# A second expert of 320 rows instead of 384, and the last stage's weight parts made beside the last experts

## The chip, the cores and the metric

One core of one Trainium2 chip runs the whole program: TensorE (PE) multiplies, VectorE (DVE), ScalarE (ACT) and GpSimd (POOL) do the rest, and SyncE (SP), ACT and POOL issue DMAs. The metric is the device time of one execution in microseconds (us); lower is better. In the profile PEld is the loading of a stationary operand, and ACTq, POOLq and SPq are the places from which DMAs are issued.

## The reference

Three layers follow one another, all in float32:

```python
# 1. attention, 2 x 8 heads, 1152 keys, 576 pooled queries, head 64
q_pool = q.reshape(B, H, S // 2, 2, D).mean(axis=3)
attn = softmax(q_pool @ k.T / sqrt(D));  x = attn @ v          # x: 1152 rows x 512
# 2. eight experts, each row goes to the one with the largest logit
e_idx = argmax(x @ w_gate);  gate_w = softmax(...)[e_idx];  eom = sigmoid(x @ w_output_gate)
for e in range(8):
    h = maximum(x[mask] @ w1[e], 0)                            # 512 -> 1024
    out[mask] = gate_w[mask] * eom[mask, e] * (h @ w2[e])      # 1024 -> 512
# 3. a gated layer
h = x @ w_in                                                   # 512 -> 2048
y = (h * tanh(softplus(h))) @ w_out                            # 2048 -> 512
```

With the inputs that the reference draws, the experts have, from the largest to the smallest, 374, 267, 240, 69, 63, 61, 51 and 27 rows.

## The kernel before

**Precision.** A product of two float32 matrices is made of three faster products (`mm3`, L1021): each operand is split into a high part `...h` and a low part `...l` (ACT copies the high part, DVE or POOL subtracts it to get the low part), and high x high, low x high and high x low are summed in PSUM. A small matrix is multiplied directly as four-byte values, without a split, in two halves of 64 columns of the array (`mm2_half`, L1039): with m = 64 rows the left half of the array makes output columns 0 to 255 and the right half 256 to 511.

**Stages.** Attention lasts to about 262 us, routing (`routing_rest`, `routing_over`) to about 285 us with the first expert begun at 278 us, then the eight experts run as "slots" one after the other to 423.5 us, and the last stage runs from 428.9 us to the end.

**Experts.** The routing ranks them by their number of rows, and `CAP` (L34) says how many groups of 64 rows the program holds for each rank: 6, 6, 4, 2, 1, 1, 1, 1. A rank with more rows than its place overflows into a loop at the end. `order` (L872) puts the ranks into slots: 0, 3, 4, 1, 5, 2, 6, 7. So slot 3 is the second largest expert (place for 384 rows), slot 5 the third (256), slots 1, 2, 4, 6 and 7 are narrow. On PE slot 3 runs from 337.3 to 372.9 us, slot 4 to 382.1, slot 5 to 406.9, slot 6 to 415.4 and slot 7 to 423.4.

A wide slot (`wide_slot`, L1105) gathers its rows in chunks of 128, transposes them, and then runs steps i = 0 to 9. Step i < 8 makes one of eight blocks of 128 hidden columns: 12 products `hps` into a PSUM buffer (there are two), of n = 384 columns in slot 3; then `relu` (L1015): ACT makes `hh` and DVE `hl`. Step i >= 2 adds, for k = i - 2, the block's part of the second layer: three products `yp` of 512 columns for each chunk of 128 rows. Two steps ahead, `w1split` (POOL makes the low part from the fourth block on) and `w2split` (ACT and DVE) split the weights into rings of four buffers, `w1h`, `w1l`, `w2h`, `w2l`; the raw weights `wt` come by four DMAs of 1 MB for an expert into five buffers. A narrow slot with 64 rows multiplies four-byte values from `wt` and splits nothing.

**Decoding and last stage.** The last stage's weights lie in memory packed and are decoded on the way (`decode_step`: DVE operations `ds`, `dm`, `wd`, an ACT copy `dm`) into 16 buffers `wd` of 1024 columns; `DECS` (L1256) says how many of these half steps follow each step of slots 0 to 4. They too are split, `wh` by ACT (`split_hi`, L1237) and the low part by DVE in place of `wd` (`split_lo`). `NPRE` = 5 of the 16 are split in slots 5 and 6, the other eleven in the last stage's steps 0 to 11.

The last stage takes three blocks of 384 rows, each in 16 steps. Step f multiplies 12 products `zps` (384 columns), evaluates the gate (ACT exp and logarithm; DVE `n`, `l`, `l`, `n`, `gl`, `n`; POOL `u`), and, four steps later (`LAG`), adds 9 products `ops` (512 columns). What each engine does in a step, and in which order, stands in the list `order_` (L1483). Between experts and last stage `turn` (L1070) brings the reloaded rows `xl<-ybuf` into PSUM, scaled by DVE (`rescale`), and `add_rows` (L1100) adds the last two experts' rows, which `pick` has prepared.

Each engine works through its own instructions in program order, and the order is that of the code: no scheduler moves anything.

Of the kernel before, what the change touches and what calls it, by code (L numbers as in the profile page):

```python
# [32 lines left out]
CAPW = 3  # L33
CAP = (6, 6, 4, 2, 1, 1, 1, 1)  # L34
# [50 lines left out]
def kernel(ctx, tc, cst, qt, kt, v, wgo, w1, w2, wio, out):  # L85
# [733 lines left out]
    astack.close()  # L819
    mstack = ExitStack()  # L820
# [101 lines left out]
    def routing_over():  # L922

        cap, nc9, ov, b8, inc = rt("cap", [8]), rt("nc9", [8, 9]), rt("ov", [8]), rt("b8", [8, 8]), rt("inc", [8])
        ts(V, cap, pi_, -1.0, ALU.mult, float(CAPW + 1), ALU.add)
        ts(V, cap, cap, float(CAPW), ALU.min, 0.0, ALU.max)

        ch, cr = rt("ch", [8]), rt("cr", [8])
        ts(V, ch, pi_, -2.0, ALU.mult, 7.0, ALU.add)
        ts(V, ch, ch, 5.0, ALU.min, 0.0, ALU.max)  # L930
# [70 lines left out]
    def split(name, w, bufs, eng):  # L1001
        hi = mp_.tile([P, 4, P], F32R, name=name + "h", bufs=bufs)
        lo = mp_.tile([P, 4, P], F32R, name=name + "l", bufs=bufs)
        act(hi, w)
        tt(eng, lo, w, hi.bitcast(F32), ALU.subtract)
        return hi, lo
# [4 lines left out]
    def w2split(s, k):  # L1011
        h_, l_ = split("w2", w2t[s, k // 4][:, k % 4].rearrange("p (a b) -> p a b", b=P), 4, V)
        w2s[s, k] = h_.rearrange("p a b -> p (a b)"), l_.rearrange("p a b -> p (a b)")

# [17 lines left out]
    def evac_half(s, y=None, r=0):  # L1032

        y = mp_.tile([P, DM], F32, name="y", bufs=3) if y is None else y
        for d in range(2):
            act(y[r:r + 64, 256 * d:256 * d + 256], ypt[s, 0][64 * d:64 * d + 64, :256])
        return y

    def mm2_half(s, k, js):  # L1039
        if k == 0:  # L1040
            ypt[s, 0] = yps.tile([P, 4, P], F32, name="yp").rearrange("p a b -> p (a b)")
        w = w2t[s, k // 4][:, k % 4]
        for d in range(2):
            mm(ypt[s, 0][64 * d:64 * d + 64, :256], lhsT=hh[s, k // 4][:, js], rhs=w[:, 256 * d:256 * d + 256], start=k == 0, stop=k == 7)

# [59 lines left out]
    def wide_slot(s, cks):  # L1105
        n = len(cks) * P

        def xprep(j):
# [3 lines left out]
            ps = xpose(cks[j], *(((yps, "yp") if s == slots[0][0] else (fp[0], f"yb{j - 1}")) if j else ()))  # L1112
            js = slice(j * P, (j + 1) * P)
# [15 lines left out]
        def main(i):  # L1129
            if i < 8:  # L1130
# [11 lines left out]
                relu(s, i, ps[:, :n], n)  # L1142
            if i >= 2:
                k = i - 2
                for j, c in enumerate(cks):
# [87 lines left out]
    NPRE = 5  # L1233
    ws2 = {}


    def split_hi(b_, f):  # L1237
        if b_ == 0:
            pool, n = (wq[0], NPRE) if f < NPRE else (zp, NF - NPRE)
            hi = pool.tile([P, 1024], F32R, name="wh", bufs=n)  # L1240
            ws2[f] = [hi]
            act(hi, wd[f])

    def split_lo(b_, f, eng=V):
        if b_ == 0:
            lo = cp.tile([P, 1024], F32R, name="wd", bufs=16) if f else wq[0].tile([P, 1024], F32R, name="wl0")
            tt(eng, lo, wd[f], ws2[f][0].bitcast(F32), ALU.subtract)
            ws2[f].append(lo)

    HB = 3  # L1250
    RL, RS = [0, 5]
# [4 lines left out]
    DECS = [[0] * 5 + [1] * 4 + [2], [0] * 5 + [1], [0] * 6, [1, 0, 0] + [1] * 7, [1] * 5 + [0]]  # L1256
# [5 lines left out]
    allc = [(c, min(P, 64 * CAP[p_])) for p_, cks in slots for c in cks]  # L1262
# [30 lines left out]
    for q, (n_, i, _, main, w_, _) in enumerate(flat):  # L1293
# [30 lines left out]
        if q > RQ and n_ < len(DECS):  # L1324
            dp_ = dq[0] if dq else scratch
            for _ in range(DECS[n_][i]):
# [6 lines left out]
        elif wq and (n_ == 5 and i % 2 or n_ == 6 and i in (2, 3)) and len(ws2) < NPRE:  # L1333
# [49 lines left out]
    def zmm(b_, f):  # L1383
        fifth = (b_, f) == steps[LAG]
        ps = zt[b_, f] = (tps if fifth else zps).tile([P, 512], F32, name="tps" if fifth else "zps")
        h_, l_ = ws2[f]
# [54 lines left out]
    def omm(b_, f):  # L1441
        h_, l_ = ws2[f]
        wo, wl_ = h_[:, 512:], l_[:, 512:]
# [34 lines left out]
    def on(i, fn):  # L1478
# [4 lines left out]
    order_ = [(-1, z_exp), (-3, z_gate), (-2, z_inv), (-3, z_hi), (-2, z_newton), (-3, z_lo), (-1, z_num), (NPRE - 1, split_lo), (NPRE, split_hi)]  # L1483
    stages = {
        0: [(NPRE, split_hi)],
# [34 lines left out]
    def over_rows(ov):  # L1520
# [38 lines left out]
        for q in range(NF // 4):  # L1559
            ps = zps.tile([P, 512], F32, name="zps")  # L1560
            for i in range(4):
                a, b_ = ws2[4 * q + i]
# [12 lines left out]
            for i in range(4):  # L1575
                a, b_ = (x_[:, 512:] for x_ in ws2[4 * q + i])
# [59 lines left out]
```

## Time and profile before

| | us |
|---|---|
| median of 3 runs (lowest, highest) | 651.24 (649.33, 652.01) |
| the profiled execution | 648.99 |
| its span on the core | 647.1 |
| PE busy in it | 618.0 |
| DVE busy | 486.1 |
| ACT busy | 396.4 |
| POOL busy | 254.5 |

The profile shows one execution. 1.9 us of its time lie outside the span. A row of the timeline gives start, duration, engine, line, operation, output and inputs; in brackets at its end stands the idle time just before it on its engine and what ended that idle time. Because matmuls are pipelined, a row's duration is longer than the distance to the next one; what a matmul costs in a full stream is read from the distance between starts.

### The profile page before, as it was taken

How to read it: one execution, taken by the hardware profiler on the slowest of the kernel's cores; microseconds unless marked ns; L12 is line 12 of the kernel's file. 1: busy time of each engine (PE TensorE's matmuls, PEld its weight loads, DVE VectorE, ACT ScalarE, POOL GpSimd, SP SyncE). 2: the span in 40 equal slices, each digit the busy share in tenths (PEclk: the TensorE clock that was granted, in tenths of full speed). 3: DMA queues.
4: the chain of work that ended last, by engine and by line, in shares of the span. 5: the costliest groups of instructions: out<-in, count | busy, mean ns of one | idle time of the engine just before them, and what ended most of it. 6: DMA issues, size and time to landing. Idle time of an engine off the chain costs nothing.

```text
span 647.1 us, 11371 instructions
## 1 busy us (share of the span) xinstructions
PE 618.0 (96%) x4144; PEld 496.3 (77%) x4144; DVE 486.1 (75%) x995; ACT 396.4 (61%) x841; POOL 254.5 (39%) x235
## 2 busy tenths in 40 slices
PE   7999999999999999589999999999999999999996
PEld 4667778787787776279868868697879999999993
DVE  4667797978787879558847778249998778878775
ACT  7789888887887675244555367346655545454453
POOL 6747638384664342242215035103223332323221
PEclk8999999999999999699999999999999999999999
DMA  6956655364451332498798496820000200000001
GB/s 248 322 152 207 174 179 125 109 189 147 120 191 34 123 86 66 132 325 305 247 389 316 172 351 238 318 81 0 2 0 1 95 5 1 2 32 18 1 0 52
DMA packets 27405, 89.86 MB, mean 139 GB/s; under 512 B 2886, under 2 KB 7631, under 8 KB 23250
## 3 DMA queue, kind: packets, MB, share of 16 engines
q1 hardware_dynamic: 22176, 74.80, 32.6%
q0 software_dynamic: 3568, 8.79, 5.9%
q10 hardware_dynamic: 1602, 5.51, 2.6%
q8 instruction: 34, 0.56, 0.4%
q14 instruction: 25, 0.20, 0.1%
HBM read 79.65 MB, written 9.97 MB: 138 GB/s over the span
## 4 chain that ended last, share of the span: by engine, by line
PE 66%; DVE 15%; ACT 7%; issue 5%; DMA 3%; POOL 2%; SPq 0%; ACTq 0%; DVEq 0%; POOLq 0%
PE pv L341 10%; PE ops L1454 8%; PE mx L237 5%; PE sc L324 5%; PE sc L322 5%; DVE l L97 4%; DVE n L97 3%; DMA wt<-in_w 3%; PE zps L1023 3%; PE pv L373 3%; PE zps L1024 3%; PE zps L1025 3%; PE yp L1023 3%; PE yp L1025 2%; PE yp L1024 2%
## 5 line engine op out<-in xcount | busy, mean ns | idle before, releaser
L100 POOL TENSOR_SCALAR u<-u 128x384 f32<-128x384 f32 x46 | 58.2, 1265 | 147.0 <-ACT u L91 147.0
L91 ACT ACTIVATE pt<-sc 128x320 f32<-128x320 f32 (+1 forms) x198 | 87.8, 490 | 10.7 <-PE sc L322 7.9
L341 PE MATMUL pv<-pt,vt 128*64 128x288 f32 x576 | 75.6, 411 | 0.0
L91 ACT ACTIVATE l<-n,two 128x384 f32<-128x384 f32 x48 | 29.6, 617 | 74.6 <-DVE n L97 74.6
L103 DVE TENSOR_REDUCE Mp<-mx 128x1 f32<-128x384 f32 x72 | 40.1, 556 | 39.6 <-PE mx L237 34.6
L324 PE MATMUL sc<-qs,at 128*128 128x320 f32 (+1 forms) x264 | 67.4, 299 | 0.0
L322 PE MATMUL sc<-qb,Bt 66*128 66x320 f32 (+1 forms) x264 | 66.6, 296 | 0.0
L1023 PE MATMUL zps<-yh,wh 128*128 128x384 f32 x184 | 63.0, 343 | 1.8 <-DVE n L97 1.8
L1025 PE MATMUL zps<-yl,wh 128*128 128x384 f32 x184 | 61.9, 337 | 0.0
L341 PEld LDWEIGHTS pv<-pt,vt 128*64 128x64 f32 x576 | 39.0, 137 | 28.5 <-issue 5.2
L1024 PE MATMUL zps<-yh,wd 128*128 128x384 f32 x176 | 59.1, 336 | 0.0
L1454 PE MATMUL ops<-wh,gl 128*128 128x512 f32 x144 | 56.9, 400 | 1.4 <-DVE gl L94 0.8
L1454 PE MATMUL ops<-wh,gh 128*128 128x512 f32 x144 | 57.2, 397 | 0.9 <-ACT gh L91 0.9
L1454 PE MATMUL ops<-wd,gh 128*128 128x512 f32 x135 | 53.2, 394 | 0.0
L100 POOL TENSOR_SCALAR dm<-dm 128x512 f32<-128x512 f32 x21 | 41.5, 1977 | 23.1 <-ACT dm L91 23.0
L94 POOL TENSOR_TENSOR Bt<-kd,at 64x576 fp32r<-64x576 f32 x32 | 45.7, 1442 | 4.2 <-ACT at L91 4.1
L324 PEld LDWEIGHTS sc<-qs,at 128*128 128x128 f32 x264 | 46.2, 189 | 1.1 <-issue 0.8
L97 DVE SCALAR_TENSOR_TENSOR l<-n,r 128x384 f32<-128x384 f32 x48 | 26.7, 556 | 25.6 <-ACT r L91 25.6
L322 PEld LDWEIGHTS sc<-qb,Bt 66*128 66x128 f32 x264 | 45.3, 189 | 0.0
L1023 PEld LDWEIGHTS zps<-yh,wh 128*128 128x128 f32 x184 | 34.6, 188 | 4.6 <-DVE n L97 3.1
L237 PE MATMUL mx<-at,qs 128*128 128x384 f32 x120 | 35.7, 363 | 2.3 <-DVE qs L94 0.8
L1053 POOL DMA_INDIRECT ybuf<-y,six x11 | 11.2, 1020 | 66.2 <-ACT y L91 48.4
(327 smaller groups left out, 1615.0 us busy)
## 6 DMA issues: line engine op xcount, KB each, us to landing
wt<-in_w SPq DMA_DIRECT2D x32, 1024.0 KB, 8.0
kd<-in_kt SPq DMA_DIRECT2D x16, 576.0 KB, 5.3
wraw<-in_wio SPq DMA_DIRECT2D x11, 512.0 KB, 4.6
wd<-in_wio SPq DMA_DIRECT2D x11, 512.0 KB, 4.1
vt<-in_v SPq DMA_DIRECT2D x8, 576.0 KB, 5.7
wraw<-in_wio ACTq DMA_DIRECT2D x7, 512.0 KB, 5.8
tq<-in_qt SPq DMA_DIRECT2D x12, 288.0 KB, 4.4
tq<-in_qt POOLq DMA_DIRECT2D x12, 288.0 KB, 6.0
```

The lines of the kernel that those rows point to most:

```text
L91: A.activation(out=out, in_=in_, func=func, **kw)
L94: eng.tensor_tensor(out=out, in0=a, in1=b, op=op)
L97: V.scalar_tensor_tensor(out=out, in0=a, scalar=s, in1=b, op0=op0, op1=op1)
L100: eng.tensor_scalar(out=out, in0=a, scalar1=s1, scalar2=s2, op0=op0, op1=op1)
L237: mm(ps, lhsT=QS[p, h][:, j * P:(j + 1) * P], rhs=keys(h), start=True, stop=True)
L322: mm(o, lhsT=Bt[(2 * p + h) % NBL][:66, ks], rhs=QB[p, h][:66, qs_], start=False, stop=last_, skip_group_check=not (first and last_))
L324: mm(o, lhsT=At[p, h][:, ks], rhs=QS[p, h][:, qs_], start=first, stop=False, skip_group_check=not (first and last_))
L341: mm(pvt[p][f][64 * h:64 * h + 64, :HQ], lhsT=vt[p][:, t, h, :], rhs=Pt[p, t][:, h, f * HQ:(f + 1) * HQ], start=t == 0, stop=t == KT - 1, ...
L1023: mm(out_, lhsT=a, rhs=c, start=first, stop=False)
L1024: mm(out_, lhsT=b_, rhs=c, start=False, stop=False)
L1025: mm(out_, lhsT=a, rhs=d, start=False, stop=last_)
L1454: mm(opt[b_, j], lhsT=(g_, g_, gl_)[i], rhs=(wo, wl_, wo)[i], start=f == 0 and i == 0, stop=f == NF - 1 and i == 2)
```

## The change

Two things are changed, and two small ones with them.

- `CAP` of the second expert goes from 6 to 5 groups of 64 rows. Slot 3 then has n = 320 columns in its first layer. Its first 256 rows go on as before. The last 64 rows get their hidden values from ACT as four-byte values `ht` (128x64 for each of eight blocks), and `mm2_tail` multiplies them with the raw weights `wt`, 16 products of 256 columns in the two halves of the array, in two groups of eight: at step i = 5 (blocks 0 to 3) and i = 9 (blocks 4 to 7). `routing_over` computes the places by the new rule.
- The rings `w1h`, `w1l`, `w2h`, `w2l` move to a pool `wsp` that outlives the experts. Of the last stage's 16 weights f, 0 to 3 are split in slot 5 and 6 into `wh` as before, 4 to 11 in slots 6 and 7 into the ring buffers, two halves of 512 columns each, and 12 to 15 in the last stage, from step 8 on (`LEAD` = 4).
- `DECS`: two of the five decode half steps of slot 4 move to steps 2 and 4 of slot 5. `RS`: `rescale` moves from step 5 to step 2 of the last slot.

```diff
-CAPW = 3
-CAP = (6, 6, 4, 2, 1, 1, 1, 1)
+CAP = (6, 5, 4, 2, 1, 1, 1, 1)
...
-        hi = mp_.tile([P, 4, P], F32R, name=name + "h", bufs=bufs)
-        lo = mp_.tile([P, 4, P], F32R, name=name + "l", bufs=bufs)
+        hi = wsp.tile([P, 4, P], F32R, name=name + "h", bufs=bufs)
+        lo = wsp.tile([P, 4, P], F32R, name=name + "l", bufs=bufs)
...
         for d in range(2):
             mm(ypt[s, 0][64 * d:64 * d + 64, :256], lhsT=hh[s, k // 4][:, js], rhs=w[:, 256 * d:256 * d + 256], start=k == 0, stop=k == 7)
+    def mm2_tail(s, j, ks):
+        if ks[0] == 0:
+            ypt[s, j] = yps.tile([P, 4, P], F32, name="yp").rearrange("p a b -> p (a b)")
+        for k in ks:
+            w = w2t[s, k // 4][:, k % 4]
+            for d in range(2):
+                mm(ypt[s, j][64 * d:64 * d + 64, :256], lhsT=ht[s][:, k], rhs=w[:, 256 * d:256 * d + 256], start=k == 0, stop=k == 7)
+
     def evac(s, j):
         y = mp_.tile([P, DM], F32, name="y", bufs=3)
         act(y, ypt[s, j])
...
                 mm(yb[i][:, k], lhsT=y[:, k * P:(k + 1) * P], rhs=pk[:, i * P:(i + 1) * P], start=False, stop=k == 3, skip_group_check=True)
     def wide_slot(s, cks):
-        n = len(cks) * P
+        n = 64 * CAP[s]
+        nf = n // P * P
         def xprep(j):
             if j == 0:
                 xh[s] = mp_.tile([P, 4, n], F32R, name="xh")
                 xl[s] = mp_.tile([P, 4, n], F32R, name="xl")
-            ps = xpose(cks[j], *(((yps, "yp") if s == slots[0][0] else (fp[0], f"yb{j - 1}")) if j else ()))
-            js = slice(j * P, (j + 1) * P)
+            m = min(P, n - j * P)
+            ps = xpose(cks[j], *(((yps, "yp") if s == slots[0][0] else (fp[0], f"yb{j - 1}")) if j else ()), m=m)[:, :, :m]
+            js = slice(j * P, j * P + m)
             act(xh[s][:, :, js], ps)
             tt(V, xl[s][:, :, js], ps, xh[s][:, :, js].bitcast(F32), ALU.subtract)
...
                                 mm(ps[:, cs_], lhsT=u[:, k], rhs=x_[s][:, k, cs_], start=u is a and x_ is xh and k == 0, stop=x_ is xl and k == 3)
                 for k in range(4) if not apart else ():
                     mm3(ps[:, :n], (a[:, k], b_[:, k]), (xh[s][:, k], xl[s][:, k]), k == 0, k == 3)
-                relu(s, i, ps[:, :n], n)
+                relu(s, i, ps[:, :nf], nf)
+                if n > nf:
+                    if i == 0:
+                        ht[s] = mp_.tile([P, 8, 64], F32, name="ht")
+                    act(ht[s][:, i], ps[:, nf:n], AF.Relu)
             if i >= 2:
                 k = i - 2
-                for j, c in enumerate(cks):
+                if n > nf and k % 4 == 3:
+                    j, c = len(cks) - 1, cks[-1]
+                    mm2_tail(s, j, range(k - 3, k + 1))
+                    if k == 7:
+                        scatter(evac_half(s, j=j), six[:64, c:c + 1], c)
+                for j, c in enumerate(cks[:nf // P]):
                     js = slice(j * P, (j + 1) * P)
                     mm2(s, j, k, hh[s, k][:, js], hl[s, k][:, js])
                     if k == 7:
...
         return [(lambda i=i: pre(i), lambda i=i: main(i), lambda: None) for i in range(-1, 6)]
     NF = FF2 // P
-    NPRE = 5
-    ws2 = {}
-
+    NWQ, NPRE, LEAD = 4, 12, 4
+    RINGS = [n_ + x_ for n_ in ("w1", "w2") for x_ in "hl"]
+    ws2, wpart = {}, {}
     def split_hi(b_, f):
-        if b_ == 0:
-            pool, n = (wq[0], NPRE) if f < NPRE else (zp, NF - NPRE)
-            hi = pool.tile([P, 1024], F32R, name="wh", bufs=n)
-            ws2[f] = [hi]
-            act(hi, wd[f])
+        if b_ or f < len(wpart):
+            return
+        if NWQ <= f < NPRE:
+            hi = [wsp.tile([P, 4, P], F32R, name=RINGS[(f - NWQ) % 2 * 2 + i], bufs=4).rearrange("p a b -> p (a b)") for i in range(2)]
+        else:
+            pool, n = (wq[0], NWQ) if f < NWQ else (zp, NF - NPRE)
+            hi = [pool.tile([P, 1024], F32R, name="wh", bufs=n)]
+        for h_, w in zip(hi, parts(wd[f], len(hi))):
+            act(h_, w)
+        wpart[f] = hi
+
+    def parts(x, n):
+        w = 1024 // n
+        return [x[:, w * i:w * i + w] for i in range(n)]
     def split_lo(b_, f, eng=V):
-        if b_ == 0:
-            lo = cp.tile([P, 1024], F32R, name="wd", bufs=16) if f else wq[0].tile([P, 1024], F32R, name="wl0")
-            tt(eng, lo, wd[f], ws2[f][0].bitcast(F32), ALU.subtract)
-            ws2[f].append(lo)
+        if b_ or f in ws2:
+            return
+        lo = cp.tile([P, 1024], F32R, name="wd", bufs=16) if f else wq[0].tile([P, 1024], F32R, name="wl0")
+        hi = wpart[f]
+        for l_, w, h_ in zip(parts(lo, len(hi)), parts(wd[f], len(hi)), hi):
+            tt(eng, l_, w, h_.bitcast(F32), ALU.subtract)
+        hi = hi if len(hi) == 2 else parts(hi[0], 2)
+        ws2[f] = list(zip(hi, parts(lo, 2)))
     HB = 3
-    RL, RS = [0, 5]
+    RL, RS = [0, 2]
     PK = 3
     LATE = 1
     XGB = 4
-    DECS = [[0] * 5 + [1] * 4 + [2], [0] * 5 + [1], [0] * 6, [1, 0, 0] + [1] * 7, [1] * 5 + [0]]
+    DECS = [[0] * 5 + [1] * 4 + [2], [0] * 5 + [1], [0] * 6, [1, 0, 0] + [1] * 7, [1] * 3 + [0] * 3, [0, 0, 1, 0, 1]]
     RQ = 2
     slots = []
     for pos_ in order:
         cks = [COL0[pos_] + j for j in range((CAP[pos_] + 1) // 2)]
         slots.append((pos_, cks))
-    allc = [(c, min(P, 64 * CAP[p_])) for p_, cks in slots for c in cks]
+    allc = [(c, min(P, 64 * CAP[p_] - P * j)) for p_, cks in slots for j, c in enumerate(cks)]
     load_w(slots[0][0], ei0, 0, (0,))
     for c, m_ in allc[:4]:
         gather(c, m_)
...
             dq.append(dstack.enter_context(tc.tile_pool(name="dq", bufs=1, side="right", reuse_waits="tile")))
         if q > RQ and n_ < len(DECS):
             dp_ = dq[0] if dq else scratch
-            for _ in range(DECS[n_][i]):
+            for _ in range(sum(DECS[n_][i:i + 1])):
                 decode_step(dp_, DEC_M)
             if n_ in (0, 4) or n_ == 3 and i > 1:
                 raw_ahead(dp_, DEC_M)
         if dec[0] == DEC_M and dq and not wq:
             dstack.close()
             wq.append(ctx.enter_context(tc.tile_pool(name="wq", bufs=1, side="right", reuse_waits="tile")))
-        elif wq and (n_ == 5 and i % 2 or n_ == 6 and i in (2, 3)) and len(ws2) < NPRE:
+        elif wq and (n_ == 5 and i % 2 or n_ == 6 or n_ == 7 and i < 4) and len(ws2) < NPRE:
             f = len(ws2)
             split_hi(0, f)
             split_lo(0, f)
...
-    order_ = [(-1, z_exp), (-3, z_gate), (-2, z_inv), (-3, z_hi), (-2, z_newton), (-3, z_lo), (-1, z_num), (NPRE - 1, split_lo), (NPRE, split_hi)]
+    order_ = [(-1, z_exp), (-3, z_gate), (-2, z_inv), (-3, z_hi), (-2, z_newton), (-3, z_lo), (-1, z_num), (LEAD - 1, split_lo), (LEAD, split_hi)]
-        0: [(NPRE, split_hi)],
+        0: [(LEAD, split_hi)],
```

First place: ACT in slot 6, from the evacuation of slot 5's last rows (`y`) on. `hl` and `hh` are the two relus of each half of the hidden layer, which in a 64-row slot PE has to wait for one after the other; `xn` and `xh` are copies of transposed rows and of the result. Before:

```order
L91 ACTIVATE y<-yp 128x512 x2
L91 ACTIVATE wh<-wd 128x1024
L91 ACTIVATE hl<-hps 128x256
L91 ACTIVATE hh<-hps 128x256
L91 ACTIVATE hl<-hps 128x256
L91 ACTIVATE hh<-hps 128x256
L91 ACTIVATE xn<-xps 128x4x64
L91 ACTIVATE xh<-yp 64x256 x2
```

After:

```order
L90 ACTIVATE y<-yp 128x512 x2
L90 ACTIVATE wh<-wd 128x1024
L90 ACTIVATE hl<-hps 128x256
L90 ACTIVATE wh<-wd 128x1024
L90 ACTIVATE hh<-hps 128x256
L90 ACTIVATE hl<-hps 128x256
L90 ACTIVATE w1h<-wd 128x512
L90 ACTIVATE w1l<-wd 128x512
L90 ACTIVATE hh<-hps 128x256
L90 ACTIVATE w2h<-wd 128x512
L90 ACTIVATE w2l<-wd 128x512
L90 ACTIVATE xn<-xps 128x4x64
```

Between `hl` and `hh` there stands now a weight copy, once `wh<-wd` of 1024 columns (f3) and once the two halves `w1h`, `w1l` of 512 (f4), and two more halves (f5) follow the second `hh`; before, there was only the one copy ahead of the first `hl`. The same goes on for f6 to f11.

Second place: DVE at the end of slot 7 (`xl<-xl,gsc` is `rescale`, `sf` and `xh<-cs,sf,gsl` are `pick`, `yl` the split of the last stage's first rows). Before:

```order
L94 TENSOR_TENSOR wd<-wd,wh 128x1024 x2
L1083 COPY gx_3592<-gix 64x1 x2
L1083 COPY sx_3593<-six 64x1 x2
L100 TENSOR_SCALAR sf<-sx_3593 128x1
L100 TENSOR_SCALAR xh<-cs,sf,gsl 128x128
L100 TENSOR_SCALAR sf<-sx_3593 128x1
L100 TENSOR_SCALAR xh<-cs,sf,gsl 128x128
L100 TENSOR_SCALAR sf<-sx_3593 128x1
L100 TENSOR_SCALAR xh<-cs,sf,gsl 128x128
L100 TENSOR_SCALAR xl<-xl,gsc 128x512 x3
```

After:

```order
L93 TENSOR_TENSOR wd<-wd,w2l 128x512
L93 TENSOR_TENSOR wd<-wd,w1h 128x512
L93 TENSOR_TENSOR wd<-wd,w1l 128x512
L99 TENSOR_SCALAR xl<-xl,gsc 128x512 x3
L93 TENSOR_TENSOR wd<-wd,w2h 128x512
L93 TENSOR_TENSOR wd<-wd,w2l 128x512
L99 TENSOR_SCALAR sf<-sx_3596 128x1
L99 TENSOR_SCALAR xh<-cs,sf,gsl 128x128
L99 TENSOR_SCALAR sf<-sx_3596 128x1
L99 TENSOR_SCALAR xh<-cs,sf,gsl 128x128
L99 TENSOR_SCALAR sf<-sx_3596 128x1
L99 TENSOR_SCALAR xh<-cs,sf,gsl 128x128
```

`rescale`, which was the last of these, stands now ahead of the low part of f11 (two rows `wd<-wd`) and of all of `pick`.

Third place: DVE in one step of the last stage, the third one (`n`, `l`, `gl` belong to the gate, `wd<-wd,wh` is the low part of a weight). Before:

```order
L97 SCALAR_TENSOR_TENSOR n<-n,zps 128x384
L97 SCALAR_TENSOR_TENSOR l<-n,r 128x384
L97 SCALAR_TENSOR_TENSOR l<-l,r 128x384
L94 TENSOR_TENSOR n<-n,l 128x384
L94 TENSOR_TENSOR gl<-n,gh 128x384
L97 SCALAR_TENSOR_TENSOR n<-u 128x384
L94 TENSOR_TENSOR wd<-wd,wh 128x1024
```

After:

```order
L96 SCALAR_TENSOR_TENSOR n<-n,zps 128x384
L96 SCALAR_TENSOR_TENSOR l<-n,r 128x384
L96 SCALAR_TENSOR_TENSOR l<-l,r 128x384
L93 TENSOR_TENSOR n<-n,l 128x384
L93 TENSOR_TENSOR gl<-n,gh 128x384
L96 SCALAR_TENSOR_TENSOR n<-u 128x384
```

The low part is gone from this step; it stands in four steps of this kind, the ninth to the twelfth or thereabouts, instead of in twelve.

## Rows read from the trace of the kernel before

**Rows 1.** Slot 3, last stage: length, busy us of PE PEld DVE ACT POOL, PEclk, DMA

```profile
347.16:372.85 25.69, 25.69 (x127) 22.49 (x127) 18.80 (x30) 9.35 (x18) 4.43 (x5) 1.00 0.59 213
440.00:490.00 50.00, 46.79 (x227) 38.78 (x227) 48.86 (x81) 30.62 (x54) 13.53 (x11) 1.00 0.00 1
```

**Rows 2.** The last stage in order of time: PE and DVE

```profile
440.78 0.50 PE L1454 MATMUL ops<-wh,gh 128*128 128x512 f32 x1 [0.43 <-ACT gh L91]
...
444.12 0.54 DVE L97 SCALAR_TENSOR_TENSOR n<-n,zps 128x384 f32<-128x384 f32 x1
...
446.84 0.50 PE L1454 MATMUL ops<-wh,gl 128*128 128x512 f32 x1 [0.83 <-DVE gl L94]
447.49 1.22 DVE L94 TENSOR_TENSOR wd<-wd,wh 128x1024 fp32r<-128x1024 f32 x1
...
448.62 0.54 DVE L97 SCALAR_TENSOR_TENSOR n<-n,zps 128x384 f32<-128x384 f32 x1
...
467.15 0.66 PE L1368 MATMUL tps<-cs,yt 128*128 128x128 f32 x4
...
489.52 0.39 PE L1454 MATMUL ops<-wh,gh 128*128 128x512 f32 x1
...
493.71 0.39 PE L1454 MATMUL ops<-wh,gh 128*128 128x512 f32 x1
```

**Rows 3.** The first steps of slot 3 in order of time

```profile
340.33 0.33 PE L1025 MATMUL hps<-xl,w1h 128*128 128x384 f32 x1
...
343.45 0.33 PE L1025 MATMUL hps<-xl,w1h 128*128 128x384 f32 x1
...
343.63 0.39 PE L1023 MATMUL yp<-w2h,hh 128*128 128x512 f32 x1
...
344.39 2.24 DVE L97 SCALAR_TENSOR_TENSOR wd<-dm,ds 128x512 int32<-128x512 int32 x1
...
344.76 1.31 POOL L94 TENSOR_TENSOR w1l<-wt,w1h 128x512 fp32r<-128x512 f32 x1
...
345.48 0.40 PE L1025 MATMUL yp<-w2l,hh 128*128 128x512 f32 x1
...
346.56 0.55 DVE L97 SCALAR_TENSOR_TENSOR hl<-hps,hh 128x384 fp32r<-128x384 f32 x1
...
347.16 0.44 PE L1023 MATMUL hps<-xh,w1h 128*128 128x384 f32 x1 [1.28 <-DVE hl L97]
```

**Rows 4.** Attention: matmuls of 320 columns in a stream

```profile
101.00 0.31 PE L324 MATMUL sc<-qs,at 128*128 128x320 f32 x1
101.15 0.31 PE L322 MATMUL sc<-qb,Bt 66*128 66x320 f32 x1
```

**Rows 5.** Slot 2: four-byte products in two halves, and what follows them

```profile
334.54 2.81 PE L1044 MATMUL yp<-wt,hh 128*64 128x256 f32 x24
337.28 0.44 PE L1023 MATMUL hps<-xh,w1h 128*128 128x384 f32 x1
```

**Rows 6.** The start of slot 5 in order of time

```profile
383.20 0.39 PE L1024 MATMUL hps<-xh,w1l 128*128 128x256 f32 x1 [0.61 <-DVE w1l L94]
...
383.98 0.69 DVE L97 SCALAR_TENSOR_TENSOR wd<-dm,ds 128x512 int32<-128x512 int32 x1
...
385.33 0.38 PE L1024 MATMUL hps<-xh,w1l 128*128 128x256 f32 x1 [0.43 <-DVE w1l L94]
...
386.69 0.63 ACT L91 ACTIVATE w2h<-wt 128x512 fp32r<-128x512 f32 x1 [1.48 <-DMA wt<-in_w]
```

**Rows 7.** Slots 6 and 7: ACT, and DVE's rescale, in order of time

```profile
407.65 1.05 ACT L91 ACTIVATE wh<-wd 128x1024 fp32r<-128x1024 f32 x1
...
412.57 0.38 ACT L91 ACTIVATE hh<-hps 128x256 f32<-128x256 f32 x1 [0.90 <-PE hps L1182]
...
422.11 1.70 DVE L100 TENSOR_SCALAR xl<-xl,gsc 128x512 f32<-128x512 f32 x3 [5.51 <-DMA xl<-ybuf]
```

**Rows 8.** Routing: a stretch with long waits of PE, same columns as rows 1

```profile
264.50:274.70 10.20, 5.56 (x38) 2.77 (x38) 6.32 (x28) 1.84 (x5) 3.55 (x4) 0.50 0.53 170
```

## What the change should do, before it was run

> **What bounds the kernel now.** I read first the busy times by stretch, then the order of time in the stretches that the change touches, and in it the bracket at a row's end: what PE waited for.
>
> PE is the bound in both stretches of [rows 1], in different ways. In slot 3, once its first steps are over, PE is busy for all 25.69 us and DVE for 18.80: there, only fewer or shorter products help. In the last stage from 440 to 490 us PE has gaps (46.79 of 50 us even though a row's duration overstates a matmul) while DVE works 48.86 of 50. So this stretch is DVE's. [Rows 2] shows its step: DVE begins a gate's `n` at 444.12 and the next at 448.62, 4.50 us apart, and PE stands 0.83 us for `gl`. Later PE's `ops` groups begin 493.71 - 489.52 = 4.19 us apart: that is PE's own step. What is in DVE's 4.50 us and not later is the low part `wd`, 448.62 - 447.49 = 1.13 us from start to start.
>
> **Last stage.** Eight of twelve `wd` leave these steps, and DVE's step becomes 4.50 - 1.13 = 3.37 us, under PE's 4.19. The gain is what PE loses there now. From the first step's `ops` at 440.78 to 489.52 lie ten steps, 48.74 us. At 4.19 they take 41.9; three of them also carry four transposes `tps`, 0.66 us at most each time, so 2.0, together 43.9. That is 4.8 us; with 0.4 for each set of transposes, since rows overstate, it is 5.6. The first wait (0.43 us, for `gh`) stays, as it waits for the first gate's chain and not for a split. The four `wd` that remain make four steps of DVE 4.50 again, 0.31 over PE's; 1.2 us in all, less than one step, while PE's first products run four steps ahead of the gate and DVE has been waiting for PE in eight steps. I cost them at nothing; if that cover is missing, they cost 1.2. I take 5.0, bounds 3.0 (the early gates still late by the chain through ACT and POOL) and 6.0.
>
> **Slot 3.** The distance of 384-column products is (343.45 - 340.33) / 18 = 0.173 us [rows 3], of 320 columns 0.15 [rows 4]: 8 x 12 = 96 products less 0.023 are 2.2 us. The third tile's 8 x 3 = 24 products of 512 columns, at (345.48 - 343.63) / 8 = 0.231 [rows 3], go: 5.55 us. What comes is 16 four-byte products. In a slot of this form each leaves two records, and 24 records take 2.81 us [rows 5]: 0.117 each, 32 for 3.75 us. Going from split products to four-byte ones and back happens four times. No row prices it alone. The product after such a group has a record of 0.44 instead of 0.33 us [rows 3, 5], 0.11 more; the bounds are 0 and 0.3 each, I take 0.15, 0.6 in all. Net 2.2 + 5.55 - 3.75 - 0.6 = 3.4 us.
>
> Not all of it reaches the end. At 347.16 PE waits 1.28 us for DVE's `hl`, which stands behind the decode's `wd` of 2.24 us [rows 3]. Ahead of that place PE saves 36 x 0.023 + 3 x 0.231 = 1.5 us. If DVE comes no sooner, this 1.5 turns into a longer wait and 1.9 us remain. If DVE's `wd` is short, as elsewhere (0.69, [rows 6]), the 1.28 goes too and 4.7 us are won. After this place DVE has 18.80 of 25.69 us to do, and the stretch would shrink by some 2 to 24: it still fits. ACT's eight extra relus `ht` (under 0.38 each, the time of 256 columns [rows 7], so 3 us at most) fit beside 9.35 us of work [rows 1]. But they are a new link: ACT's `ht` follows DVE's `hl` on the same PSUM buffer, so ACT's next copies stand behind DVE's queue, decode included, and PE's product two steps on needs `ht` to be done. I take 2.6 us, between 1.9 and 3.4, with bounds 1.0 (that link costs 0.9) and 4.7.
>
> Whether `wd` is long or short is where the Trainium skill differs from the trace. The row: `wd` began at 344.39, POOL's `w1l` at 344.76, and `wd` ended 0.56 us after POOL's end at 346.07 [rows 3]. The Trainium skill ("SBUF — State Buffer", section "SBUF: two separate sides") says DVE and GpSimd take a common pair of ports for a whole instruction, and that whichever starts first has it while the other stands fully blocked. That one of them stands agrees with the trace (2.24 against 0.69 us); that the first wins does not, since `wd` started first and stood. By the page `wd` would have kept 0.69 us and slot 3 would give the 4.7 of the bound.
>
> **Slots 4 and 5.** PE's two waits for `w1l`, 0.61 and 0.43 us [rows 6], came behind decode work that now comes later. But ACT's `w2h` waits until 386.69 for a DMA, so that PE's second layer cannot begin sooner unless the transfer does; the raw `wt` buffers of slot 3 are held longer now, by the second tail group. Gain 0 to 1.0. The two decode half steps now stand in slot 5, each with at least a `wd` of 0.69 us ahead of an `hl`: up to -1.4. I take +0.3.
>
> **Slots 6 and 7.** Here ACT has 0.90 us free before a relu [rows 7], and a split of 1.05 us, or two halves of 0.63 us (the 512-column copy in [rows 6]), goes in between: late by 0.15 or 0.36. Six relus have such a copy ahead. PE has products of the other half to go on with in part; I take -0.6, bounds 0 and -2.2. DVE is idle there (5.51 us before `rescale`), so the low parts cost nothing. `rescale` moves ahead of f11's low part (1.22) and of `pick`; it waits for the reload's DMA, and `pick` is needed only after the reloaded rows' products: nothing, or up to 2.9 (1.70 + 1.22) if PE stood for it. Five more tiny DVE operations in `routing_over` lie beside the first expert's products: nothing.
>
> **Sum.** 5.0 + 2.6 + 0.3 - 0.6 = 7.3 us. The profiled execution's 648.99 (span 647.1 and 1.9 around it) becomes 641.7. It lies 2.25 us, 0.35%, under the median of the runs, which is what the new time is compared with: 651.24 - 7.3 = 643.9 us. 0.5% is 3.3 us, about the least that a measurement of this kernel tells from no change.
>
> **Rivals.**
> A. Only the last stage gives: slot 3's saving ends in the wait for `hl` and in ACT's new link, slot 5's in its DMA. For: the 1.28 us wait is there already. Against: from 347.16 on PE has no gap. Gain 5.0, 646.2 us. Chance 0.2.
> B. Everything gives: 5.6 + 4.7 + 1.0 = 11.3, 639.9 us. For: `ht` holds ACT back and with it POOL's `w1l`, so `wd` may stay free. Chance 0.15.
> C. The last stage's step is set by the gate's chain DVE-ACT-DVE and not by DVE's load; the waits stay and only 0 to 1 us is won there, with 2.3 elsewhere: 648.4. For: `gl` waits for `gh`. Against: later the same chain runs at 4.19 us. Chance 0.1.
> D. Slower: ACT's splits in slots 6 and 7 make each of the eight relus late by their whole length, 2 x 0.63: 8 x 1.26 = 10.1 us against a gain of 7.9 elsewhere, 653.4 us. It decides from 1.0 us a relu. For: PE's transposes wait for each relu. Against: 0.90 us of ACT's time is free there. Chance 0.08. In routing, where PE did 5.56 us of work in 10.20, the granted clock was 0.50, 1.2 GHz [rows 8]; in the stretches of [rows 1], with waits under 1 us, it was 1.00. The Trainium skill ("TensorE: Matmul & The Clock Gate", section "HAM oscillation — how this bites in real kernels") says that a PE which waits between short bursts falls back to the low clock every time; by that D would lose up to another 5 us, an estimate from half of the 10.20.
> E. The change doesn't do what it says: over 320 rows the second expert would run in the overflow loop. It has 267; chance 0.
>
> **How the numbers follow.** The forecast has 0.47, its own range 641 to 647. A and B are faster too; with a few hundredths of the forecast and of A below 3.3 us of gain, faster is 0.80. C and that rest make 0.12 for within 0.5%, D makes 0.08 slower. The range, 639.6 to 649.3, reaches over A, B and C and leaves out D and the ends.
>
> **What would show it.** Last stage: `ops` groups 4.2 us apart from the first steps on, PE's waits for `gl` gone, DVE below 45 us of 50; if the steps stay 4.5, C. Slot 3: first `hps` to slot 4's first product 2 to 3.5 us shorter than 35.6 (372.9 - 337.3), `yp<-wt,ht` near 1.9 us for each group; a wait over 1.28 us for `hl` or `ht` means A, none means B. Slots 6 and 7: together at most 1 us longer than 16.5; more means D. I am wrong if the time is above 649 or the gain comes from elsewhere, say from DMAs that land sooner.

## The result and the profile after

The changed kernel takes 643.9 us (median of 6 runs, 642.96 to 645.37) against 650.3 us before (6 runs); the ratio is 0.9901, 95% interval 0.9882 to 0.992, so 6.4 us less. The median is the forecast's 643.9. Its terms are not the forecast's: two were too high and one too low, and that the sum agrees all the same is luck, as the section on the prediction works out below.

This table shows where the profiled executions differ: the distance on PE from the first product of each part to the first of the next. "To first ops" is the stretch from the last stage's first `zps` to its first `ops` group, and the last column is the ten steps from the first to the eleventh `ops` group. e1 to e5 are experiments told below.

| us | slot 0 | 1 | 2 | 3 | 4 | 5 | 6 | 7 | turn | to first ops | ten steps |
|---|---|---|---|---|---|---|---|---|---|---|---|
| before | 36.04 | 13.30 | 10.01 | 35.66 | 9.27 | 24.84 | 8.39 | 8.05 | 5.42 | 11.87 | 48.75 |
| after | 35.53 | 13.41 | 9.96 | 31.22 | 9.31 | 26.04 | 8.39 | 8.52 | 5.42 | 11.52 | 46.64 |
| e1 splits only | 36.14 | 13.41 | 10.01 | 35.59 | 9.27 | 24.71 | 8.39 | 8.52 | 5.42 | 11.54 | 46.65 |
| e2 other order | 35.48 | 13.41 | 9.97 | 31.22 | 9.31 | 26.29 | 8.39 | 8.61 | 5.42 | 11.27 | 43.16 |
| e4 ht first | 35.32 | 13.41 | 9.96 | 34.37 | 9.27 | 25.41 | 8.39 | 8.52 | 5.42 | 11.53 | 46.66 |
| e5 six buffers | 36.72 | 13.42 | 9.97 | 31.21 | 9.31 | 23.20 | 8.39 | 8.51 | 5.42 | 11.27 | 45.42 |

Slot 3 gave 4.4 us, the last stage 2.1 in the ten steps and 0.35 before them; slot 5 took 1.2 back and slot 7 0.5. Slot 0 lies between 35.3 and 36.7 us in these profiles, in kernels with the same code there, so its 0.5 is not counted. (In the longest, e5's, the granted clock was 0.50, or 1.2 GHz, from 279 to 281 us.)

Two stretches of the profile after that answer to [rows 1], with the same columns: slot 3 behind its first wait, and 440 to 490 us in the last stage.

```profile
345.83:369.34 23.51, 23.51 (x138) 18.90 (x138) 15.37 (x28) 11.39 (x29) 6.07 (x5) 1.00 0.62 217
...
440.00:490.00 50.00, 48.12 (x241) 42.01 (x241) 44.93 (x80) 27.03 (x52) 14.54 (x12) 1.00 0.00 1
```

PE is still busy for all of slot 3's stretch, and it is shorter. In the last stage DVE fell from 48.86 to 44.93 us of 50, though five of the nine splits in this stretch, 1.22 us each, are gone (seven of the eleven in the stage; the prediction said eight of twelve, one too many in each), and PE rose only from 46.79 to 48.12.

**Slot 3.** The same instructions as in [rows 3], and one of the two tail groups, in the order of time after:

```profile
338.38 0.31 PE L1030 MATMUL hps<-xh,w1l 128*128 128x320 f32 x1
...
342.42 1.30 POOL L93 TENSOR_TENSOR w1l<-wt,w1h 128x512 fp32r<-128x512 f32 x1 [0.90 <-ACT w1h L90]
...
343.37 0.31 PE L1031 MATMUL hps<-xl,w1h 128*128 128x320 f32 x1
...
344.49 0.69 DVE L96 SCALAR_TENSOR_TENSOR wd<-dm,ds 128x512 int32<-128x512 int32 x1
345.10 0.42 DVE L96 SCALAR_TENSOR_TENSOR hl<-hps,hh 128x256 fp32r<-128x256 f32 x1
345.55 0.22 ACT L90 ACTIVATE ht<-hps 128x64 f32<-128x64 f32 x1 [2.94 <-DVE hl L96]
...
345.83 0.42 PE L1029 MATMUL hps<-xh,w1h 128*128 128x320 f32 x1 [0.76 <-ACT ht L90]
...
346.90 1.30 POOL L93 TENSOR_TENSOR w1l<-wt,w1h 128x512 fp32r<-128x512 f32 x1 [2.04 <-ACT w1h L90]
...
353.86 0.31 PE L1031 MATMUL hps<-xl,w1h 128*128 128x320 f32 x1
...
354.10 1.95 PE L1058 MATMUL yp<-wt,ht 128*64 128x256 f32 x16
355.98 0.50 PE L1029 MATMUL yp<-w2h,hh 128*128 128x512 f32 x1
356.31 0.40 PE L1030 MATMUL yp<-w2h,hl 128*128 128x512 f32 x1
```

`wd` takes 0.69 us where it took 2.24. POOL's second `w1l` of this place, which ran into it before, now starts at 346.90, because ACT's copy for it stands behind `ht`, and `ht` behind DVE's `hl` (2.94 us idle). PE waits 0.76 us instead of 1.28, and now for `ht`. Products of 320 columns are (343.37 - 338.38) / 34 = 0.1468 us apart. A tail group takes 355.98 - 354.10 = 1.88 us; the product ahead of it and the one behind it last 0.09 and 0.10 longer than in a stream (0.24 for 0.147, 0.33 for 0.231).

**Slot 5.** The start of the slot (378.65) to the second layer's first product:

```profile
379.74 0.39 PE L1030 MATMUL hps<-xh,w1l 128*128 128x256 f32 x1 [0.71 <-DVE w1l L93]
...
384.37 0.63 ACT L90 ACTIVATE w2h<-wt 128x512 fp32r<-128x512 f32 x1 [2.64 <-DMA wt<-in_w]
...
385.05 0.50 PE L1029 MATMUL yp<-w2h,hh 128*128 128x512 f32 x1 [0.95 <-ACT w2h L90]
```

One of the two waits for `w1l` of [rows 6] is gone, but `w2h` begins 5.72 us into the slot; before, 386.69 - 382.21 = 4.48. PE now stands for it.

**Slot 7.** Here a relu, `hl`, comes late behind ACT's new weight copies:

```profile
416.17 0.44 PE L1207 MATMUL hps<-cs,hl 128*128 128x128 f32 x2 [0.33 <-ACT hl L90]
```

Before, PE did not stand at this place. In slot 6 it still does not.

**The last stage.** One of the first steps, DVE, ACT and PE:

```profile
440.42 0.54 DVE L96 SCALAR_TENSOR_TENSOR n<-u 128x384 f32<-128x384 f32 x1
...
441.00 0.62 ACT L90 ACTIVATE l<-n,two 128x384 f32<-128x384 f32 x1 [2.14 <-DVE n L96]
441.65 0.52 ACT L90 ACTIVATE r<-l 128x384 f32<-128x384 f32 x1
...
442.20 0.56 DVE L96 SCALAR_TENSOR_TENSOR l<-n,r 128x384 f32<-128x384 f32 x1 [0.78 <-ACT r L90]
...
444.05 0.55 DVE L93 TENSOR_TENSOR gl<-n,gh 128x384 fp32r<-128x384 f32 x1
444.52 0.55 DVE L96 SCALAR_TENSOR_TENSOR n<-u 128x384 f32<-128x384 f32 x1
...
444.66 0.51 PE L1491 MATMUL ops<-wh,gl 128*128 128x512 f32 x1 [0.58 <-DVE gl L93]
```

From one `n<-u` to the next are 444.52 - 440.42 = 4.10 us, not 3.37. DVE's work fell as forecast, but DVE now stands 0.78 us in each step for ACT's `r`. ACT makes `r` from `l`, and `l` from DVE's `n<-u`. On DVE, the next `n<-u` stands behind what `r` feeds. So the way goes from DVE to ACT, back to DVE and on to the next `n<-u`: a loop through two engines, each in program order, that takes 4.10 us. Before, the low part `wd` stood on DVE between `n<-u` and `l<-n,r` and filled this time.

### The profile page after: what moved, and what is told of

Same layout as the page of the kernel before. It is cut to its first block, busy times and chain, and to the rows that moved or that the text cites. A ratio compares the mean times of both kernels' runs of the same rounds, so it can differ in the third digit from the quotient of the medians.

```text
span 643.6 us, 11433 instructions
## 1 busy us (share of the span) xinstructions
PE 614.1 (95%) x4152; PEld 491.2 (76%) x4152; DVE 487.3 (76%) x1006; ACT 396.0 (62%) x858; POOL 254.3 (40%) x235
## 4 chain that ended last, share of the span: by engine, by line
PE 67%; DVE 15%; ACT 8%; issue 4%; DMA 3%; POOL 1%; ACTq 0%; DVEq 0%; POOLq 0%
PE pv L340 10%; PE ops L1491 8%; PE mx L236 5%; PE sc L321 5%; PE sc L323 5%; DVE l L96 4%; PE zps L1029 3%; PE pv L372 3%; PE zps L1030 3%; PE zps L1031 3%; PE yp L1029 2%; PE yp L1031 2%; PE yp L1030 2%; DVE n L96 2%; ACT l L90 2%
## 5 line engine op out<-in xcount | busy, mean ns | idle before, releaser
L93 DVE TENSOR_TENSOR w2l<-wt,w2h 128x512 fp32r<-128x512 f32 x32 | 24.9, 785 | 14.8 <-ACT w2h L90 13.8
L93 DVE TENSOR_TENSOR n<-n,l 128x384 f32<-128x384 f32 x48 | 34.8, 725 | 1.7
L93 DVE TENSOR_TENSOR st<-pt 128x1152 f32<-128x1152 f32 x25 | 34.0, 1358 | 2.7 <-ACT pt L90 2.7
L250 DVE CUSTOM_DVE_ANT_0 wd<-mx,wd 128x384 f32<-128x384 f32 x63 | 34.6, 549 | 1.2 <-ACT wd L90 0.7
L90 ACT ACTIVATE wd<-mx 128x384 f32<-128x384 f32 x63 | 28.7, 497 | 10.4 <-PE mx L236 6.0
```

What stands on the lines that cost most here:

```text
L90: A.activation(out=out, in_=in_, func=func, **kw)
L93: eng.tensor_tensor(out=out, in0=a, in1=b, op=op)
L250: V.tensor_tensor_reduce(out=r_, in0=ps, in1=r_, scale=1.0, scalar=-3.0e38, op0=ALU.add, op1=ALU.max, accum_out=Mp[p % 2][:, h, j, 1:2])
```

## The experiments

Two questions were open: why slot 3 gave more than forecast, and where the rest of the last stage's gain and slot 5's loss come from. Each kernel was timed beside the kernel before on the same chip (647.8 to 649.8 us there), e6 in a single run. The changed kernel itself was not timed again on these chips.

**e1.** The changed kernel with the row count of before, and with it routing's rule of before for the places.

```diff
-CAP = (6, 5, 4, 2, 1, 1, 1, 1)
+CAPW = 3
+CAP = (6, 6, 4, 2, 1, 1, 1, 1)
...
```

> The changed kernel with 384 rows again for the second expert: only the weights' splits, the two decode half steps and the earlier rescale are as changed. Theory H (the raw weights are held longer): slot 5 lost 1.2 us in the changed kernel because the second group of four-byte products holds a raw weight buffer, so here, without that group, slot 5 takes 24.8 us or less as in the kernel before; slot 3 takes 35.7 again; the last stage keeps its gain of 2.5 us; time about 648.5 us, 2 us under the kernel before. Rival D (decode): the two decode half steps in slot 5 cost the 1.2 us, and slot 5 takes 26.0 here too; time about 649.5.

Measured: 645.5 us against 647.84, ratio 0.9965 (0.9952 to 0.9978). Slot 3 takes 35.59 us, the ten steps 46.65, slot 7 8.52, slot 5 24.71. So the last stage's gain belongs to the splits, and so does slot 7's loss (PE waits 0.33 us for the same relu), and the two decode half steps, with what they give back in slot 4 and the wait for `w1l`, cost slot 5 nothing in sum: this run's rival D falls. The other 4 us, with slot 5's loss in them, belong to the rows.

**e2.** The changed kernel with another order of one step.

```diff
-order_ = [... (-2, z_inv), (-3, z_hi), (-2, z_newton), (-3, z_lo), (-1, z_num), ...]
+order_ = [... (-2, z_inv), (-3, z_hi), (-1, z_num), (-3, z_lo), (-2, z_newton), ...]
```

> The changed kernel with another order of one step in the last stage: DVE does the Newton operations (l, l, n of the step before) after gl and after the next step's n instead of ahead of them, so that it need not stand for ACT's l and r. Theory L (the step is a loop DVE-ACT-DVE of 4.1 us, just under PE's 4.19, so DVE builds up no lead): PE's waits for gl in the first two steps (1.3 us) and in the four steps with splits (about 1.9) go, the eleven ops groups lie 2 to 3 us closer, 641 to 642 us. Rival W (DVE's work itself, or POOL's u, sets the step): no change, 643.9, or slower by a fraction because gh and gl come later.

Measured: 639.34 us against 647.84, ratio 0.9873 (0.9855 to 0.989). Its repetitions e8 and e10 gave 0.9854 (0.9838 to 0.987) and 0.9879 (0.9857 to 0.9901). The ten steps take 43.16 us and the PE is busy in all of them. The stretch from the first to the eleventh `ops` group of the changed kernel, and of e8:

```profile
438.53:485.17 46.64, 44.75 (x222) 38.71 (x223) 41.74 (x73) 25.37 (x48) 13.84 (x11) 1.00 0.00 1
```

```profile
437.48:480.64 43.16, 43.16 (x224) 39.03 (x224) 41.01 (x71) 24.76 (x48) 12.98 (x11) 1.00 0.00 1
```

DVE does nearly the same work in both (41.74 and 41.01 us). Only the order differs, and 3.5 us go. One step of e2 on DVE:

```profile
441.97 0.55 DVE L96 SCALAR_TENSOR_TENSOR n<-n,zps 128x384 f32<-128x384 f32 x1
...
443.59 0.86 DVE L96 SCALAR_TENSOR_TENSOR l<-n,r 128x384 f32<-128x384 f32 x1
...
445.68 0.56 DVE L96 SCALAR_TENSOR_TENSOR n<-n,zps 128x384 f32<-128x384 f32 x1
```

DVE no longer stands for `r`, and its step is 445.68 - 441.97 = 3.71 us instead of 4.10. Theory L stands: the loop, not the work, held the step. The new order also puts `gl` ahead of the three Newton operations, so it comes sooner within its step; how much of the early waits went by that and how much by the shorter step, this run does not tell. At the stage's end, from the 41st `ops` group to the last product, it saves another 1.0 us (24.5 instead of 25.5). The whole time shows less of it: by the ratios e2 lies 0.2 to 0.5% under the changed kernel's 0.9901, 1.4 to 3.1 us, and slot 5 is longer in its profiles (26.29, in e8 27.02, in e10 27.43) than the 26.04 of the changed kernel.

**e7.** The same order in the kernel before.

```diff
-order_ = [... (-3, z_hi), (-2, z_newton), (-3, z_lo), (-1, z_num), (NPRE - 1, split_lo), ...]
+order_ = [... (-3, z_hi), (-1, z_num), (-3, z_lo), (-2, z_newton), (NPRE - 1, split_lo), ...]
```

> The kernel before with e2's order of the step. Theory L: there DVE's own work (4.5 us a step with a split in it) is the bound and the loop is not, so the order gives little: the ten steps 48.0 to 48.75 us instead of 48.75, the time at most 0.7 us lower. Rival W2 (the loop with ACT sets the steps there too): the ten steps fall by 2 us or more.

Measured: 647.49 us against 648.5, ratio 0.999 (0.9974 to 1.0005). The ten steps take 49.42 us, 0.7 more than expected at the most, but the first `ops` group comes 0.6 us sooner (11.28 us instead of 11.87), so that the eleventh comes at the same time. With a split in each step the work is the bound there, and the order does not matter. Only when the splits had left did the loop come to the front. At the stage's end the order saves 1.0 us here too. Slot 7, which has the code of before in this kernel, took 8.73 us instead of 8.05, with 0.47 us of PE's waiting for a load of `wt`; so the length of slot 7 alone does not show a loss of 0.5, and the row of the late relu has to.

**e6.** The changed kernel without the low parts of the last four weights.

```diff
+        if f >= NPRE:
+            ws2[f] = list(zip(parts(hi[0], 2), parts(hi[0], 2)))
+            return
```

> The changed kernel without the low parts of the last four weights (their high part is multiplied in their place, so this part of the computation is changed). Theory L (a loop of 4.1 us leaves no lead, so each remaining split costs PE about its excess): the ten steps go from 46.64 to about 45 us and the first two steps keep their waits. The prediction's view (the four are covered by a lead): 46.6 us as before.

Measured: the ten steps take 44.72 us, 1.9 less than after (46.64); the wait for `gl` in the second step is still there.

```profile
446.14 0.50 PE L1494 MATMUL ops<-wh,gl 128*128 128x512 f32 x1 [0.59 <-DVE gl L93]
```

So the four splits that I had costed at nothing cost 1.9 us, and the early waits the other 1.6 of e2's 3.5. That is also more than the 1.2 that the prediction gave if the cover were missing; two of the four splits share their step with the next block's `yl` of 0.68 us, which its working left out. The whole time (644.79, one run) tells nothing here, since slot 5 (27.27) and slot 7 (9.79) were long in this profile: in slot 5 PE stood 1.99 us for `w2h` and the granted clock was then 0.50 from 385 to 388 us, and in slot 7 PE stood 1.05 us for a load of `wt`.

**e4.** The changed kernel with `ht` ahead of `hh`.

```diff
-                relu(s, i, ps[:, :nf], nf)
                 if n > nf:
...
                     act(ht[s][:, i], ps[:, nf:n], AF.Relu)
+                relu(s, i, ps[:, :nf], nf)
```

> The changed kernel with ACT's ht ahead of hh, so that ht no longer follows DVE's hl. Theory C (ht's wait for hl is what held POOL's w1l back and kept DVE's wd at 0.69 us in slot 3): now ACT runs ahead again, POOL's w1l falls on wd, wd takes over 2 us and PE's wait in slot 3's first steps grows from 0.76 to 1.3 us or more; slot 3 31.2 to 32 us. Rival K (ht is itself the late link): the wait shrinks by ht's 0.3 us or more, slot 3 takes under 31.2 us.

Measured: 646.96 us against 647.84, ratio 0.998 (0.9963 to 0.9996). Slot 3 takes 34.37 us, over 3 us more than in the changed kernel, and more than theory C had put. The rows at the same place:

```profile
344.80 2.21 DVE L96 SCALAR_TENSOR_TENSOR wd<-dm,ds 128x512 int32<-128x512 int32 x1
...
345.18 1.28 POOL L93 TENSOR_TENSOR w1l<-wt,w1h 128x512 fp32r<-128x512 f32 x1
...
346.94 0.41 DVE L96 SCALAR_TENSOR_TENSOR hl<-hps,hh 128x256 fp32r<-128x256 f32 x1
...
347.40 0.42 PE L1029 MATMUL hps<-xh,w1h 128*128 128x320 f32 x1 [2.37 <-DVE hl L96]
```

Freed from `hl`, ACT runs ahead, POOL's `w1l` falls on `wd` again, `wd` takes 2.21 us and PE waits 2.37. The new wait of `ht`, which I had counted as a risk, is what keeps `wd` short; rival K falls. The longer wait is 1.6 of the 3.15 us that slot 3 lost. The rest is TensorE's clock, which was at 0.50 (1.2 GHz) after PE had stood:

```profile
348.00:351.00 3.00, 3.00 (x12) 2.90 (x12) 2.59 (x3) 0.41 (x3) 1.10 (x1) 0.50 0.95 369
```

In this stretch the products of 320 columns are 0.267 us apart instead of 0.147; the first 15 products behind the wait take 4.11 us where the changed kernel, at 1.00, needs 2.56.

**e3.** The changed kernel with both tail groups one step earlier.

```diff
-                if n > nf and k % 4 == 3:
+                if n > nf and k % 4 == 2:
...
-                    mm2_tail(s, j, range(k - 3, k + 1))
-                    if k == 7:
+                    mm2_tail(s, j, range(k - 2, k + 2))
+                    if k == 6:
```

> The changed kernel with both groups of four-byte products one step earlier (i = 4 and i = 8). Theory H: slot 5's first weight is released and sent about 1.4 to 3 us sooner, its second layer's first weight lands sooner, and slot 5 gets 0.5 to 1.2 us shorter: 642.7 to 643.4 us. Rival D: slot 5 stays at 26.0 us. Against both: the first group may stand for ht of block 3, which ACT has only just made, up to 1 us.

Measured: 643.67 us against 647.84, ratio 0.9944 (0.9923 to 0.9964). Slot 5 takes 29.59 us, the opposite of what both theories said. But the profiled execution took 647.26 us, 3.6 more than the median, so this profile does not show what slot 5 takes in most executions.

```profile
384.90 0.63 ACT L90 ACTIVATE w2h<-wt 128x512 fp32r<-128x512 f32 x1 [5.08 <-DMA wt<-in_w]
...
385.58 0.79 PE L1029 MATMUL yp<-w2h,hh 128*128 128x512 f32 x1 [3.38 <-ACT w2h L90]
```

The slot's first load was issued sooner (11.5 us ahead of the slot instead of 10.8), but its second-layer weight landed 7.2 us into the slot instead of 5.7. From 374 to 382 us the DMA engines are busy for all of the stretch here, and behind PE's wait the granted clock was 0.50:

```profile
374.00:382.00 8.00, 8.00 (x70) 6.54 (x66) 5.05 (x9) 3.85 (x9) 0.94 (x1) 1.00 1.00 376
```

```profile
386.00:391.00 5.00, 5.00 (x19) 4.38 (x19) 4.81 (x6) 3.24 (x8) 4.43 (x3) 0.50 0.70 267
```

The clock is some 2.4 us of the slot's 3.55 over the changed kernel: the first 20 products behind the wait take 6.13 us here and 3.75 there. For the landing, the release alone does not set it; the packed weights for the decode and the gathered rows are on their way in the same microseconds. Which of them slows which is open.

**e5.** e2 with six buffers for raw weights.

```diff
-            w[s, k] = mp_.tile([P, 4, 512], F32, name="wt", bufs=5)
+            w[s, k] = mp_.tile([P, 4, 512], F32, name="wt", bufs=6)
...
-    NWQ, NPRE, LEAD = 4, 12, 4
+    NWQ, NPRE, LEAD = 2, 10, 4
```

> The kernel of e2 with six buffers for raw weights instead of five; to make room two weights fewer are split beside the last experts (10 of 16, six left to the last stage). Theory H (slot 5 is late because a raw weight buffer held by the four-byte products delays its loads into traffic that is already there): slot 5's first load is issued in slot 3 with a second one behind it, and slot 5 falls from 26.3 us to 24.8 or less; the two more splits in the last stage cost under 0.3 us in e2's order; 637.5 to 638 us on a chip where e2 has 639.3. Rival Q (it is the transfers themselves, the same bytes through the same queues, that end late): slot 5 stays at 26 us, 639 to 640.

Measured: 638.78 us against 648.5, ratio 0.985 (0.9834 to 0.9865), the same as e8's 0.9854 on that chip. Slot 5:

```profile
379.07:402.27 23.20, 23.20 (x151) 20.39 (x149) 18.40 (x25) 14.60 (x29) 8.09 (x6) 1.00 0.84 309
```

PE has no gap in it. It is 3.1 us less than e2's 26.29, 3.8 less than e8's 27.02 (where the granted clock was 0.50 from 384 to 386 us, behind a wait of 1.94) and 1.6 less than before. A sixth buffer takes the wait away, as theory H says: the load that `w2h` waits for, slot 5's third, goes out 7.3 us ahead of the slot (at 371.75 us), where it was 4.5 in the changed kernel (374.18) and 5.0 before (377.18). That the tail group holds its buffer is only a part of the cause. It delays slot 5's first load, which goes out at 367.86 us in the changed kernel, while DVE's split, the last reader of these weights before, is done at 367.21: some 0.6 us. Yet that load goes out 10.8 us ahead of slot 5 instead of 13.6, and the third then takes 10.2 us until ACT can begin `w2h`, instead of 9.5. Most of the 2.8 us is slot 3's own gain: less work lies between this place and slot 5. And the two weights more that the last stage has to split cost 45.42 - 43.16 = 2.3 us there, where I had expected 0.3.

**e9 and e11** tried to keep e5's slot 5 without that price: e9 with three gathered chunks instead of four and five weights left to the last stage, e11 with the six splits four steps sooner. Both edits are shown against e5.

```diff
-    XGB = 4
+    XGB = 3
...
-    NWQ, NPRE, LEAD = 2, 10, 4
+    NWQ, NPRE, LEAD = 3, 11, 4
...
```

> e5 with room made otherwise: three gathered chunks of rows are held instead of four, and 11 of the 16 weights are split beside the last experts, so that five are left to the last stage. Theory: slot 5 stays at 23.2 us as in e5, the ten steps fall from e5's 45.4 to 44.2 or less (e2 with four has 43.2), slot 0 to 3 as in e5 unless a gather now comes late; 0.983 of the kernel before. Rival: the missing chunk costs a wait at the start of a slot, 0.985 or more.

```diff
-    NWQ, NPRE, LEAD = 2, 10, 4
+    NWQ, NPRE, LEAD = 2, 10, 8
```

> e5 with the last stage's six splits begun four steps sooner (steps 2 to 7 instead of 6 to 11), so that they no longer stand in the steps that also subtract the next block's rows (yl). Theory: six splits at 0.3 us over PE's step are covered by DVE's lead if nothing else comes in these steps; the ten steps fall from e5's 45.4 to 43.2 to 43.8, slot 5 stays at 23.2, 0.982 of the kernel before. Rival: there is no lead yet in steps 2 to 7, the six cost as much there, 45 us or more, 0.985.

e9: ratio 0.9909 (0.9886 to 0.9932); slot 5 has 23.20 us and the ten steps 44.24 as expected, but slot 2 takes 14.20 instead of 9.97: the chunk comes late, as its rival said. PE stood 2.49 us for it, and the granted clock was 0.50 from 339 to 342 us behind that. e11: ratio 0.9859 (0.9836 to 0.9882); slot 5 24.05, the ten steps 46.13, so the six splits cost as much in the first steps, as its rival said: DVE's step is 4.59 us there, PE runs on through four of them and then stands 1.53 us for DVE's `n`. e10 was e2 beside e9.

> The kernel of e2 again, beside e5 and e7 on one chip: 0.987 of the kernel before, slot 5 at 26.3 us, the ten steps at 43.2.

> The kernel of e2 beside e9 on one chip: 0.986 of the kernel before, slot 5 at 26 to 27 us, the ten steps at 43.2.

e2 (with e8 and e10), e5 and e11 are the fastest versions, 1.2 to 1.5% under the kernel before; these runs do not rank them.

## Why the prediction was right in the sum and wrong in three terms

- **Last stage, 5.0 forecast, 2.5 measured (2.1 and 0.35).** The step that failed is "DVE's step becomes 4.50 - 1.13 = 3.37 us". I took DVE's load for its pace. In the rows of before DVE had no idle time, and what it would wait for without the splits could not be seen in its own rows; but the order of the step, with ACT's `r` between two DVE operations, was there to be read. The loop is 4.10 us, so DVE gains 0.09 us a step on PE's 4.19 instead of 0.82. With that the cover of the four splits goes too ("DVE has been waiting for PE in eight steps"): they cost 1.9 us (e6), not 0. Rival C named the loop, but said that the waits would stay and only 0 to 1 us be won; the loop is just under PE's step, and 2.1 were.
- **Slot 3, 2.6 forecast, 4.4 measured.** The products are near the sum: 96 x (0.1733 - 0.1468) = 2.5 us, the third tile 5.55, the tail groups 2 x (1.88 + 0.19) = 4.1 against 3.75 + 0.6. That is 3.95 for a forecast of 3.4. The larger part, 1.3 of the 1.8, is the wait: I took 0.8 off for it, and it got 0.5 us shorter. Rival B named the mechanism, `ht` holding back POOL's `w1l`, and e4 shows it by taking it away.
- **Slots 4 and 5, +0.3 forecast, -1.2 measured.** The longer hold of the raw weights was in the working, but only as a limit on the gain, and I gave no price to it; that slot 3's gain brings slot 5 nearer to its loads was not in it at all. e5 shows that the late load had a price.
- **Slots 6 and 7, -0.6 forecast, -0.5 measured**, all in slot 7. Rival D, every relu late, did not come: of the six relus with a copy ahead one made PE stand, 0.33 us, and the granted clock stayed at 1.00 in both slots. `rescale` ahead of `pick` cost nothing: turn and added rows take 5.42 us as before.
- The four errors sum to -2.5 + 1.8 - 1.5 + 0.1 = -2.1 us, so the terms give 5.2 us in the two profiles; the medians differ by 6.4, with an interval from 5.2 to 7.7, and the forecast was made from a median of 651.24 where six runs give 650.3. The two profiled executions differ by only 3.6 us (648.99 and 645.37): in the one after, slot 0 begins 1.3 us later (279.22 instead of 277.92; in all the profiles it begins between 277.3 and 279.4) and the end comes 0.9 us later behind the last product. The central value was reached by luck; that it lay on the right side was not, since slot 3's and the last stage's gains were each there.
- **Which of `wd` and `w1l` stands.** e4 repeats what [rows 3] showed: `wd` began before POOL's `w1l` (344.80 and 345.18) and it was `wd` that stood.

## What to carry to other kernels

When an engine's load is taken out of a step, its new pace is not the load that is left: follow one value through all engines in their program order, and if it comes back to the first engine within the same step, that loop can be the pace until the order is changed. When a stage gets shorter, the next stage's loads are needed sooner, but their buffers come free only with their last reader; look up when that is and what else is on its way then. A long wait of PE can cost more than itself, so read the granted clock behind it. And a new wait on a helper engine can also help, by moving another engine out of the way.

## What was not expected of the hardware

- Two engines can collide by when they start, with the same work. DVE's `wd` (128x512) takes 0.69 us alone and 2.21 to 2.24 us when POOL's 1.3 us subtraction starts 0.37 or 0.38 us after it, in the kernel before and in e4.
- A load that is issued sooner can land later: in e3's profile slot 5's second-layer weight was issued 5.0 us ahead of the slot instead of 4.5, and came 1.4 us later in it (7.2 us against 5.7), with the DMA engines busy for 1.00 of the stretch from 374 to 382 us.
- TensorE's clock did not follow the length of PE's wait. In slot 5, with the same code there, it fell to 0.50 for about 3 us behind waits of 1.94 (e8), 1.99 (e6) and 2.10 us (e10), and stayed at 1.00 behind one of 2.18 (e2). The first eleven products behind the wait took 3.64 us in e8 and 2.48 in e2.
